# Retention and a squared-ReLU feed-forward on one core: feed-forward on one 128-token unit, and an order from a list schedule

## The chip, the core and the metric

The kernel runs on one core of a Trainium2 chip. The metric is the device time of one execution in microseconds (us), the median of several runs. The core's engines work through their own instruction streams in order: TensorE (PE, with weight loads shown apart as PEld), VectorE (DVE), ScalarE (ACT), GpSimd (POOL) and SyncE (SP), which issues the loads from memory. They wait for one another by semaphores.

## The reference

The input holds q, k and v of 8 batches, 8 heads, 576 positions and 64 dimensions, and two weight matrices. The first half is causal retention with a decay per head, the second a feed-forward with squared ReLU:

```python
scores = q @ k.T / sqrt(64)                    # per batch and head
ret = scores * where(i >= j, gamma[h] ** (i - j), 0)
x = (ret @ v), heads side by side              # 4608 tokens x 512
h = x @ w_in                                   # 512 x 2048
out = max(h, 0) ** 2 @ w_out                   # 2048 x 512, float32 out
```

The kernel casts to float16 for the matmuls and sums in float32.

## The kernel before, in words

The 4608 tokens are cut into 36 units of 128. Of each batch, units c = 0 to 3 are chunks of 128 positions ("full"); the last 64 positions of two batches share a "tail" unit. So five units in nine are: four of one batch, four of the next and a tail, with 8 full units of c = 0, 24 others and 4 tails.

**Retention of a unit.** The loads of q, k, v (L69, tails L72) are 256 KB each. `cast_unit` casts k on POOL (L171) and q on DVE for units 0 to 7, on POOL for later ones (L172), and multiplies v by a decay on POOL (L175). On PE, `steps_T` transposes k and q with 4 matmuls each of 128 columns (L191) into one PSUM tile, `psT`; after the last of the 8, ACT copies k to `kTb` in two halves (L196, L197) and DVE copies q to `qT` (L198). `steps_score` makes 8 score matmuls (L215) and DVE applies the mask in two operations (L218). `steps_state` (4 matmuls, L240) carries the state R from chunk to chunk (DVE: L246 for c = 0, else L249 and L250). `steps_out` multiplies scores with v (8 matmuls, L268) and adds the state's share (none for c = 0, 4 matmuls for other full units, 8 of 64 columns for a tail, L274); DVE scales it into `xT` (L281). All of these matmuls have 128 or 64 moving columns and a weight load of their own.

**Feed-forward of a group.** Four units make a group of 512 tokens. `steps_ff1` takes each of 16 slices f of the hidden dimension: 4 matmuls of 512 columns (L301) into one PSUM bank `ph`, then ReLU on ACT (L306) and the square on DVE (L307) into `gT`. `steps_ff2` takes each unit of the group: 16 matmuls of 512 columns (L326) into `po`, a copy on ACT (L330) and the store, issued by ACT (L333). `ph` and `po` share three PSUM banks.

**What sets the order.** The tile pools keep the program's order on each engine (`manual_schedule`). The retention of units 0 to 3 runs first, one unit after another; then the four blocks of w_in are cast on DVE (`cast_w`, L97) while the loads of w_out wait for the four staging buffers that these casts free; then the feed-forward of group 0 runs, with the casts of w_out ahead of its second half; then the retention of units 4 to 7, one after another. From group 1 on, the loop at the end puts one or two retention steps of the units of the next group behind each feed-forward matmul, at phases written by hand (`SLOT`, `late`). Constants (`lnrow`, `gam`, masks) are made at the start; DVE also clears `bdec` and three sets of `vp` and `kTb` (L156, L159, L160) before its first cast of q.

Of the kernel before, what the change touches and what calls it, by code (L numbers as in the profile page):

```python
# [11 lines left out]
ALU = mybir.AluOpType  # L12


@with_exitstack
def kernel(
# [43 lines left out]

    loaded = {}

    def load(u):
        kind, b, c = units[u]
        t = {}
        for name, src in (("q", q), ("k", k), ("v", v)):
            x = ld.tile([P, H, D], FP32, name=f"{name}32", tag=f"{name}32")
            if kind == "full":
                nc.sync.dma_start(out=x, in_=src[b, :, c * P:(c + 1) * P, :].rearrange("h p d -> p h d"))  # L69
            else:  # L70
                for i in range(2):
                    nc.sync.dma_start(out=x[i * 64:(i + 1) * 64],  # L72
                                      in_=src[b + i, :, 512:576, :].rearrange("h p d -> p h d"))
            t[name] = x
        loaded[u] = t
# [4 lines left out]
    NLD = 6  # L80
    for u in range(UPG):
        load(u)
    w_st = []
    for fb in range(4):
        t = stage.tile([P, NP, 512], FP32, name=f"wi{fb}", tag="wst")
        nc.sync.dma_start(out=t, in_=w_in[:, fb * 512:(fb + 1) * 512].rearrange("(m p) f -> p m f", p=P))
        w_st.append(t)

    def load_w_out(fb):
        t = stage.tile([P, 4, DM], FP32, name=f"wo{fb}", tag="wst")  # L90
        nc.sync.dma_start(out=t, in_=w_out[fb * 512:(fb + 1) * 512, :].rearrange("(n p) m -> p n m", p=P))
        w_st.append(t)

    def cast_w(i):
        fb = i % 4
        dst = w_in16[:, :, fb * 512:(fb + 1) * 512] if i < 4 else w_out16[:, fb * 4:(fb + 1) * 4, :]
        nc.vector.tensor_copy(out=dst, in_=w_st[i])  # L97
# [53 lines left out]
    NB = 3  # L151
# [12 lines left out]
    ret = {}  # L164

    def cast_unit(u):
        kind = units[u][0]
        t = loaded.pop(u)
        k16 = cast.tile([P, H * D], FP16, name="k16", tag="k16")
        q16 = cast.tile([P, H * D], FP16, name="q16", tag="q16")  # L170
        nc.gpsimd.tensor_copy(out=k16, in_=t["k"].rearrange("p h d -> p (h d)"))  # L171
        (nc.vector if u < 2 * UPG else nc.gpsimd).tensor_copy(out=q16, in_=t["q"].rearrange("p h d -> p (h d)"))  # L172
        vp = vps[u % NB]
        vo = vp.rearrange("p n (a d) -> p n a d", d=64)[:, :, 0:3:2, :]
        nc.gpsimd.tensor_tensor(  # L175
            out=vo,
            in0=t["v"].rearrange("p (n a) d -> p n a d", a=2),
            in1=vdec[kind].rearrange("p (n a o) -> p n a o", a=2, o=1).to_broadcast([P, NP, 2, D]),
            op=ALU.mult)
        ret[u] = {"k16": k16, "q16": q16, "vp": vp}  # L180

    def steps_T(u):
        r = ret[u]
        steps = []
        for i, src in enumerate(("k16", "q16")):
            for hp in range(NP):
                def f(i=i, src=src, hp=hp):
                    if i == 0 and hp == 0:
                        r["psT"] = ps_one.tile([P, 2, NP, P], FP16, name="psT", tag="psT")
                    ps = r["psT"]  # L190
                    nc.tensor.transpose(ps[:, i, hp, :], r[src][:, hp * P:(hp + 1) * P], ident)  # L191
                    if hp == NP - 1:
                        if i == 1:
                            kT = kTs[u % NB]
                            qT = work.tile([P, NP, P], FP16, name="qT", tag="qT")
                            nc.scalar.copy(out=kT[0:64, :, 0, :], in_=ps[0:64, 0])  # L196
                            nc.scalar.copy(out=kT[64:128, :, 1, :], in_=ps[64:128, 0])  # L197
                            nc.vector.tensor_copy(out=qT, in_=ps[:, 1])  # L198
                            r["kT"], r["qT"] = kT, qT
                steps.append(f)  # L200
        return steps

    def steps_score(u):
        kind = units[u][0]
        r = ret[u]
        steps = []
        for hp in range(NP):
            for a in range(2):
                def f(hp=hp, a=a):
                    if hp == 0 and a == 0:  # L210
                        r["rT"] = work.tile([P, NP, 2, P], FP16, name="rT", tag="rT")
                    rT = r["rT"]
                    if hp % 2 == 0 and a == 0:
                        r["psc"] = ps_sc.tile([P, 2, 2, P], FP32, name="psc", tag="psc")
                    nc.tensor.matmul(r["psc"][:, hp % 2, a, :], lhsT=r["kT"][:, hp, a, :],  # L215
                                     rhs=r["qT"][:, hp, :], start=True, stop=True)
                    if hp % 2 == 1 and a == 1:
                        nc.vector.tensor_tensor(  # L218
                            out=rT[:, hp - 1:hp + 1].rearrange("p n a i -> p (n a) i"),
                            in0=r["psc"].rearrange("p n a i -> p (n a) i"),  # L220
                            in1=mask[kind].rearrange("p (o i) -> p o i", o=1).to_broadcast([P, 4, P]),
                            op=ALU.mult)
                steps.append(f)
        return steps

    R = {}

    def steps_state(u):
        kind, b, c = units[u]
        if kind == "tail":  # L230
            return []
        r = ret[u]
        steps = []
        for hp in range(NP):
            def f(hp=hp):
                if hp == 0:
                    r["psS"] = ps_one.tile([P, NP, 2, D], FP32, name="psS", tag="psS")
                ps = r["psS"]
                vo = r["vp"].rearrange("p n (a d) -> p n a d", d=64)[:, hp, 0:3:2, :]
                nc.tensor.matmul(ps[:, hp], lhsT=r["k16"][:, hp * P:(hp + 1) * P], rhs=vo,  # L240
                                 start=True, stop=True)
                if hp == NP - 1:
                    psf = ps.rearrange("p n a d -> p n (a d)")
                    Rn = st_pool.tile([P, NP, P], FP16, name="R", tag="R")
                    if c == 0:
                        nc.vector.tensor_tensor(out=Rn, in0=psf, in1=bdec, op=ALU.mult)  # L246
                    else:
                        tmp = work.tile([P, NP, P], FP32, name="stmp", tag="stmp")
                        nc.vector.tensor_tensor(out=tmp, in0=psf, in1=R[b], op=ALU.add)  # L249
                        nc.vector.tensor_tensor(out=Rn, in0=tmp, in1=bdec, op=ALU.mult)  # L250
                    r["Rn"] = Rn
            steps.append(f)
        return steps

    xTs = {}

    def steps_out(u):
        kind, b, c = units[u]
        r = ret[u]
        g, s = divmod(u, UPG)  # L260
        inter = [] if c == 0 else ([(0, P, R[b])] if kind == "full" else [(0, 64, R[b]), (64, P, R[b + 1])])
        steps = []
        for hp in range(NP):
            for a in range(2):
                def f(hp=hp, a=a):
                    if hp == 0 and a == 0:
                        r["psO"] = ps_one.tile([P, NP, P], FP32, name="psO", tag="psO")
                    nc.tensor.matmul(r["psO"][:, hp, :], lhsT=r["vp"][:, hp, a * 64:a * 64 + P],  # L268
                                     rhs=r["rT"][:, hp, a, :], start=(a == 0),
                                     stop=(a == 1 and not inter))  # L270
                steps.append(f)
            for i, (lo, hi, Rb) in enumerate(inter):
                def f(hp=hp, lo=lo, hi=hi, Rb=Rb, last=(i == len(inter) - 1)):
                    nc.tensor.matmul(r["psO"][:, hp, lo:hi], lhsT=Rb[:, hp, :], rhs=r["qT"][:, hp, lo:hi],  # L274
                                     start=False, stop=last)
                steps.append(f)
# [153 lines left out]
```

## Time and profile before

| | |
|---|---|
| median of 3 runs | 373.37 us |
| the runs | 371.81, 373.37, 375.94 us |
| the profiled execution | 375.74 us, its span 374.0 us |
| mean granted TensorE clock | 0.938 |
| DMA | 46.52 MB, 36.70 MB read, mean 124 GB/s |

The span is the time from the first to the last instruction of the profiled execution. A line of a timeline begins with the start, then the time that the merged instructions took together, the engine, the line of the kernel, and the number of instructions; brackets hold the idle time ahead of it and what ended it. A line of a table of stretches gives for each engine the busy time and, in brackets, the number of instructions, then the granted TensorE clock (1.00 is full), the busy share of the DMA engines and GB/s. Matmuls are pipelined: the distance between the starts of two tells what one costs in a run of them, not its own length.

### The profile page before, as it was taken

Reading aid. Unit: us, or ns where it says so; the run is one execution under the profiler, and the core shown is the slowest. Engines: PE = TensorE matmul, PEld = TensorE weight load, DVE = VectorE, ACT = ScalarE, POOL = GpSimd, SP = SyncE. Lnnn points to the kernel's source line nnn. Section 1 sums busy time; section 2 is a strip of 40 time slices with the busy share of each in tenths; the row PEclk is TensorE's granted clock in tenths of the full one; section 3 lists DMA queues with packets and bytes.
Section 4 is the critical chain, followed back from the end, with each engine's and each line's share of the span. In section 5 each row is a group of like instructions: output and inputs, shape, how many; then the busy total and the mean of one; then the engine's idle time right before and its main releaser. Section 6 shows DMA issues by size and latency. Waiting matters only on the chain.

```text
span 374.0 us, 5968 instructions
## 1 busy us (share of the span) xinstructions
PE 332.7 (89%) x2272; PEld 186.3 (50%) x2272; DVE 207.1 (55%) x401; ACT 151.4 (40%) x259; POOL 84.1 (22%) x113
## 2 busy tenths in 40 slices
PE   0565979654899999999999999999999999999995
PEld 0453434344555555555555555555555555555442
DVE  5477565174468547645744784485368637832400
ACT  3211540312164256435632652465356236523621
POOL 4500024042323222223222322222223222000000
PEclk9986798955599999999999999999999999999999
DMA  9990999598985554555355436545300020011012
GB/s 175 253 358 9 359 256 190 172 220 148 222 142 113 154 154 94 116 141 133 86 124 151 119 86 142 150 104 118 109 29 2 28 58 28 2 58 58 0 53 60
DMA packets 122012, 46.52 MB, mean 124 GB/s; under 512 B 113280, under 2 KB 113280, under 8 KB 121984
## 3 DMA queue, kind: packets, MB, share of 16 engines
q1 hardware_dynamic: 116736, 36.71, 45.3%
q10 hardware_dynamic: 5248, 9.44, 7.3%
q8 instruction: 17, 0.28, 0.3%
q14 instruction: 11, 0.09, 0.1%
HBM read 36.70 MB, written 9.44 MB: 123 GB/s over the span
## 4 chain that ended last, share of the span: by engine, by line
PE 84%; DVE 10%; ACT 4%; issue 1%; ACTq 0%
PE ph L301 34%; PE po L326 34%; PE psc L215 5%; PE psT L191 4%; PE psO L268 4%; DVE rT L218 2%; PE psS L240 2%; ACT kTb L197 1%; ACT kTb L196 1%; DVE xT L281 1%; PE psO L274 1%; DVE R L250 1%; DVE qT L198 1%; DVE stmp L249 1%; DVE q L172 1%
## 5 line engine op out<-in xcount | busy, mean ns | idle before, releaser
L301 PE MATMUL ph<-xT,w_in 128*128 128x512 f16 x576 | 155.9, 389 | 3.3 <-DVE w_in L97 2.2
L326 PE MATMUL po<-w_out,gT 128*128 128x512 f16 x576 | 150.9, 383 | 2.6 <-DVE w_out L97 2.4
L306 ACT ACTIVATE rl<-ph 128x512 f16<-128x512 f32 x144 | 85.7, 597 | 60.4 <-PE ph L301 54.0
L307 DVE TENSOR_TENSOR gT<-rl 128x512 f16<-128x512 f16 x144 | 67.3, 472 | 48.3 <-ACT rl L306 47.5
L301 PEld LDWEIGHTS <-w_in 128*128 128x128 f16 x576 | 55.9, 100 | 53.4 <-issue 7.4
L326 PEld LDWEIGHTS <-gT 128*128 128x128 f16 x576 | 55.0, 99 | 52.0 <-DVE w_out L97 2.9
L215 PE MATMUL psc<-qT,kTb 128*128 128x128 f16 x288 | 55.9, 234 | 14.8 <-DVE qT L198 14.8
L330 ACT COPY o<-po 128x512 f32<-128x512 f32 x36 | 21.1, 586 | 108.6 <-PE po L326 107.0
L175 POOL TENSOR_TENSOR vp<-v,vdec_full 128x512 f16<-128x512 f32 x32 | 36.2, 1133 | 106.6 <-PE psO L274 45.3
L198 DVE COPY qT<-psT 128x512 f16<-128x512 f16 x36 | 15.3, 425 | 66.6 <-ACT kTb L197 66.6
L218 DVE TENSOR_TENSOR rT<-psc,mask_full 128x512 f16<-128x512 f32 x64 | 43.0, 685 | 9.5 <-PE psc L215 9.5
L171 POOL CAST k<-k 128x512 f16<-128x512 f32 x36 | 23.2, 644 | 108.9 <-DMA k<-in_k_dram 53.0
L268 PE MATMUL psO<-rT,vp 128*128 128x128 f16 x288 | 46.9, 236 | 0.6 <-DVE rT L218 0.6
L196 ACT COPY kTb<-psT 64x512 f16<-64x512 f16 x36 | 20.8, 579 | 47.8 <-PE psT L191 44.9
L215 PEld LDWEIGHTS <-kTb 128*128 128x128 f16 x288 | 28.1, 105 | 19.3 <-ACT kTb L196 7.9
L268 PEld LDWEIGHTS <-vp 128*128 128x128 f16 x288 | 29.5, 106 | 14.9 <-issue 1.1
L191 PE MATMUL psT<-ident,q 128*128 128x128 f16 x144 | 20.3, 234 | 9.4 <-DVE q L172 9.4
L274 PE MATMUL psO<-qT,R 128*128 128x128 f16 (+1 forms) x128 | 27.0, 230 | 0.0
L191 PE MATMUL psT<-ident,k 128*128 128x128 f16 x144 | 20.7, 238 | 6.0 <-POOL k L171 6.0
L240 PE MATMUL psS<-vp,k 128*128 128x128 f16 x128 | 25.8, 240 | 0.0
L191 PEld LDWEIGHTS <-k 128*128 128x128 f16 x144 | 14.5, 108 | 17.0 <-POOL k L171 6.0
L191 PEld LDWEIGHTS <-q 128*128 128x128 f16 x144 | 13.6, 104 | 17.5 <-DVE q L172 11.1
(47 smaller groups left out, 170.3 us busy)
## 6 DMA issues: line engine op xcount, KB each, us to landing
q<-in_q_dram SPq DMA_DIRECT2D x32, 256.0 KB, 3.6
k<-in_k_dram SPq DMA_DIRECT2D x32, 256.0 KB, 4.5
v<-in_v_dram SPq DMA_DIRECT2D x32, 256.0 KB, 4.1
out_dram<-o ACTq DMA_DIRECT2D x32, 256.0 KB, 2.3
wi<-in_moe_w_in_dram SPq DMA_DIRECT2D x4, 1024.0 KB, 9.1
wo<-in_moe_w_out_dram SPq DMA_DIRECT2D x4, 1024.0 KB, 8.6
q<-in_q_dram SPq DMA_DIRECT2D x8, 128.0 KB, 3.7
k<-in_k_dram SPq DMA_DIRECT2D x8, 128.0 KB, 3.9
```

Source lines behind the costliest of these rows:

```text
L175: nc.gpsimd.tensor_tensor(out=vo, in0=t["v"].rearrange("p (n a) d -> p n a d", a=2), in1=vdec[kind].rearrange("p (n a o) -> p n a o", a=2, ...
L191: nc.tensor.transpose(ps[:, i, hp, :], r[src][:, hp * P:(hp + 1) * P], ident)
L196: nc.scalar.copy(out=kT[0:64, :, 0, :], in_=ps[0:64, 0])
L215: nc.tensor.matmul(r["psc"][:, hp % 2, a, :], lhsT=r["kT"][:, hp, a, :], rhs=r["qT"][:, hp, :], start=True, stop=True)
L218: nc.vector.tensor_tensor(out=rT[:, hp - 1:hp + 1].rearrange("p n a i -> p (n a) i"), in0=r["psc"].rearrange("p n a i -> p (n a) i"), in1= ...
L240: nc.tensor.matmul(ps[:, hp], lhsT=r["k16"][:, hp * P:(hp + 1) * P], rhs=vo, start=True, stop=True)
L268: nc.tensor.matmul(r["psO"][:, hp, :], lhsT=r["vp"][:, hp, a * 64:a * 64 + P], rhs=r["rT"][:, hp, a, :], start=(a == 0), stop=(a == 1 and ...
L274: nc.tensor.matmul(r["psO"][:, hp, lo:hi], lhsT=Rb[:, hp, :], rhs=r["qT"][:, hp, lo:hi], start=False, stop=last)
L301: nc.tensor.matmul(cur["ph"], lhsT=w_in16[:, m, f * P:(f + 1) * P], rhs=xTs[g][:, m, :], start=(m == 0), stop=(m == NP - 1))
L306: nc.scalar.activation(out=rl, in_=cur["ph"], func=ACTF.Relu)
L307: nc.vector.tensor_tensor(out=gT[f], in0=rl, in1=rl, op=ALU.mult)
L326: nc.tensor.matmul(po[t], lhsT=gT[f][:, t * P:(t + 1) * P], rhs=w_out16[:, f, :], start=(f == 0), stop=(f == NF - 1))
```

## The change

The feed-forward works on one unit of 128 tokens instead of a group of four. FFN1 of a unit takes four slices f into the four quarters of one PSUM bank, so each of its matmuls has 128 moving columns instead of 512 and there are 2304 of them instead of 576; ReLU and square still take 512 columns at a time, four of each per unit. FFN2 is the same 16 matmuls of 512 columns per unit.

All of the work after the constants is given as tasks to a new class, `Schedule`: each has an engine, a key, a duration, tasks that it depends on, and counted resources that it takes (PSUM banks, buffers). `emit` plays an event simulation with these durations and a latency per engine; whenever an engine is free it starts the ready task with the smallest key whose resources are there. The order of the starts is the program's order. Keys are places in units of 32 feed-forward slots: the feed-forward of unit u lies at 32u, its retention from 32(u - 1) - 17.6 on. The simulation starts with all engines free at time 0; the constants are not in it.

Other edits: loads go k, q, v; the order of the loads is units 0 to 3, the eight weight blocks, units 4 and on. Staging has 5 buffers instead of 4, the loads of units 5 instead of 6, `vp` and `kTb` 4 instead of 3, and other pools change size. Each weight block is cast half on DVE and half on ACT, with a key ahead of nearly all other work. The copies of k wait for the transposes of k alone. q is cast on DVE for units 0 to 3 only. The bodies of the retention's instructions are as before. The core of the diff:

```diff
+class Schedule:
+    LAT = {"PE": 0.25, "ACT": 0.12, "DVE": 0.12, "POOL": 0.15, "SP": 2.0}
+    def __init__(self, count):
+        self.count = dict(count)
+        self.tasks = []
+    def add(self, eng, key, dur, fn, deps=(), acq=(), after=None):
+        t = dict(eng=eng, key=key, dur=dur, fn=fn, acq=acq, n=len(self.tasks), users=[], free=[],
+                 left=len(deps), ready=0.0, lat=self.LAT[eng] if after is None else after)
+        for d in deps:
+            d["users"].append(t)
+        self.tasks.append(t)
+        return t
+    def free(self, res, tasks):
+        group = dict(res=res, left=len(tasks))
+        for t in tasks:
+            t["free"].append(group)
...
+            for e in ready:
+                if busy[e]:
+                    continue
+                held = []
+                while ready[e]:
+                    item = heapq.heappop(ready[e])
+                    t = item[2]
+                    if all(self.count[r] > 0 for r in t["acq"]):
+                        for r in t["acq"]:
+                            self.count[r] -= 1
+                        t["start"] = now
+                        order.append(t)
+                        busy[e] = True
+                        push(now + t["dur"], "end", t)
+                        break
+                    held.append(item)
...
+                if what == "end":
+                    busy[t["eng"]] = False
+                    for w in t["users"]:
+                        push(now + (0.0 if w["eng"] == t["eng"] else t["lat"]), "dep", w)
+                    for g in t["free"]:
+                        push(now + t["lat"], "free", g)
...
+        for t in order:
+            t["fn"]()
...
-    UPG = 4
-    NG = NU // UPG
     const = ctx.enter_context(tc.tile_pool(name="const", bufs=1))
-    ld = ctx.enter_context(tc.tile_pool(name="ld", bufs=6))
-    stage = ctx.enter_context(tc.tile_pool(name="stage", bufs=4))
-    cast = ctx.enter_context(tc.tile_pool(name="cast", bufs=3))
-    work = ctx.enter_context(tc.tile_pool(name="work", bufs=2))
-    st_pool = ctx.enter_context(tc.tile_pool(name="st", bufs=4))
-    g_pool = ctx.enter_context(tc.tile_pool(name="g", bufs=2))
+    ld = ctx.enter_context(tc.tile_pool(name="ld", bufs=5))
+    stage = ctx.enter_context(tc.tile_pool(name="stage", bufs=5))
+    cast = ctx.enter_context(tc.tile_pool(name="cast", bufs=4))
+    work = ctx.enter_context(tc.tile_pool(name="work", bufs=3))
+    o_pool = ctx.enter_context(tc.tile_pool(name="o", bufs=2))
+    x_pool = ctx.enter_context(tc.tile_pool(name="x", bufs=5))
+    st_pool = ctx.enter_context(tc.tile_pool(name="st", bufs=6))
+    g_pool = ctx.enter_context(tc.tile_pool(name="g", bufs=16))
     r_pool = ctx.enter_context(tc.tile_pool(name="r", bufs=3))
     ps_ff = ctx.enter_context(tc.tile_pool(name="ps_ff", bufs=3, space=bass.MemoryType.PSUM))
...
-    NB = 3
+    NB = 4
...
+    sched = Schedule(dict(ph=2, po=1, psc=2, psT=1, psS=1, psO=1, ld=5, wst=5, k16=4, q16=4,
+                          qT=3, rT=3, x=5, g=4, rl=3, o=2, R=6))
+    add = sched.add
+    tile_of = {}
+    last_load = []
+    def dma_task(key, dur, fn, **kw):
+        t = add("SP", key, dur, fn, deps=list(last_load), **kw)
+        last_load[:] = [t]
+        return t
...
+        for n, (name, src) in enumerate((("k", k), ("q", q), ("v", v))):
+            def fn(name=name, src=src):
...
+            loaded[name, u] = dma_task(0, 1.22, fn, acq=("ld",) if n == 0 else ())
+    def add_weight(i):
+        fb = i % 4
...
+        t = dma_task(0, 2.75, fn, acq=("wst",))
+        dst = w_in16[:, :, fb * 512:(fb + 1) * 512] if i < 4 else w_out16[:, fb * 4:(fb + 1) * 4, :]
+        halves = []
+        for j, eng in enumerate(("DVE", "ACT")):
+            def fc(j=j, eng=eng):
+                s = tile_of["w", i]
+                (nc.vector.tensor_copy if eng == "DVE" else nc.scalar.copy)(
+                    out=dst[:, 2 * j:2 * j + 2], in_=s[:, 2 * j:2 * j + 2])
+            halves.append(add(eng, -50 + i, 0.65 if eng == "DVE" else 1.0, fc, deps=[t]))
+        sched.free("wst", halves)
+        wcast[i] = halves
+    ahead = 4
+    for u in range(ahead):
+        add_load(u)
+    for i in range(8):
+        add_weight(i)
+    for u in range(ahead, NU):
+        add_load(u)
+    T = {}
+    L = 2 * NF
+    def add_ret(u):
+        kind, b, c = units[u]
+        base = (u - 1) * L
...
+        ck = add("POOL", base - L, 0.73, fk, deps=[loaded["k", u]], acq=("k16",))
+        if u < ahead:
+            cq = add("DVE", base - L, 0.42, fq, deps=[loaded["q", u]], acq=("q16",))
+        else:
+            cq = add("POOL", base - L + 1, 0.62, fq, deps=[loaded["q", u]], acq=("q16",))
+        cv = add("POOL", base - L + 2, 1.1, fv, deps=[loaded["v", u]] + ([T["out", u - NB]] if u >= NB else []))
+        sched.free("ld", [ck, cq, cv])
...
+        tk = add("PE", base - 17.6, 0.22, ft(0, "k16"), deps=[ck], acq=("psT",))
+        tq = add("PE", base - 15.6, 0.22, ft(1, "q16"), deps=[cq, tk])
+        sched.free("q16", [tq])
+        kT = kTs[u % NB]
...
+        prev = [T["score", u - NB]] if u >= NB else []
+        e0 = add("ACT", base - 15.5, 0.58, fe0, deps=[tk] + prev)
+        e1 = add("ACT", base - 15.4, 0.58, fe1, deps=[tk] + prev)
+        eq = add("DVE", base - 15.3, 0.42, feq, deps=[tq], acq=("qT",))
+        sched.free("psT", [e0, e1, eq])
...
+            s = add("PE", base + 0.5, 0.22, fs, deps=[ck, cv], acq=("psS",))
+            sched.free("k16", [s, tk])
...
+                sc.append(add("PE", base + 5 + 2 * half + j + 0.6, 0.11, f, deps=[e0, e1, eq] + sc[-1:],
+                              acq=("psc",) if j == 0 else ()))
...
+            ms.append(add("DVE", base + 7 + 2 * half, 0.7, fm, deps=[sc[-1]] + ms[-1:],
+                          acq=("rT",) if half == 0 else ()))
+            sched.free("psc", [ms[-1]])
...
+            outs.append(add("PE", base + 18.5 + hp, 0.16, f,
+                            deps=[ms[hp // 2], cv] + [T["R", ru] for _, _, ru in inter] + outs[-1:],
+                            acq=("psO",) if hp == 0 else ()))
...
+        T["x", u] = add("DVE", base + 22.6, 0.7, fx, deps=[outs[-1]], acq=("x",))
+        sched.free("psO", [T["x", u]])
+        T["out", u] = outs[-1]
...
+    def add_ff(u):
+        base = u * L
+        f1 = []
+        sq = []
+        for fb in range(4):
+            for j in range(4):
+                def f(fb=fb, j=j):
+                    if j == 0:
+                        tile_of["ph", u, fb] = ps_ff.tile([P, 4, P], FP32, name="ph", tag="ff")
+                    fi = 4 * fb + j
+                    for m in range(NP):
+                        nc.tensor.matmul(tile_of["ph", u, fb][:, j, :], lhsT=w_in16[:, m, fi * P:(fi + 1) * P],
+                                         rhs=tile_of["x", u][:, m, :], start=(m == 0), stop=(m == NP - 1))
+                acq = ()
+                if j == 0:
+                    acq = ("ph", "g") if fb == 0 else ("ph",)
+                f1.append(add("PE", base + 4 * fb + j, 0.216, f, deps=[T["x", u]] + wcast[fb] + f1[-1:], acq=acq))
+            def fr(fb=fb):
+                t = tile_of["rl", u, fb] = r_pool.tile([P, 4, P], FP16, name="rl", tag="rl")
+                nc.scalar.activation(out=t, in_=tile_of["ph", u, fb], func=ACTF.Relu)
+            def fg(fb=fb):
+                t = tile_of["g", u, fb] = g_pool.tile([P, 4, P], FP16, name="gT", tag="gT")
+                rl = tile_of["rl", u, fb]
+                nc.vector.tensor_tensor(out=t, in0=rl, in1=rl, op=ALU.mult)
+            r = add("ACT", base + 4 * fb + 4, 0.6, fr, deps=[f1[-1]], acq=("rl",))
+            sched.free("ph", [r])
+            sq.append(add("DVE", base + 4 * fb + 6, 0.45, fg, deps=[r]))
+            sched.free("rl", [sq[-1]])
+        sched.free("x", [f1[-1]])
+        f2 = []
+        for fi in range(NF):
+            def f(fi=fi):
+                if fi == 0:
+                    tile_of["po", u] = ps_ff.tile([P, DM], FP32, name="po", tag="ff")
+                nc.tensor.matmul(tile_of["po", u], lhsT=tile_of["g", u, fi // 4][:, fi % 4, :], rhs=w_out16[:, fi, :],
+                                 start=(fi == 0), stop=(fi == NF - 1))
+            f2.append(add("PE", base + NF + fi, 0.216, f, deps=[sq[fi // 4]] + wcast[4 + fi // 4] + f2[-1:],
+                          acq=("po",) if fi == 0 else ()))
+        sched.free("g", [f2[-1]])
...
+        oc = add("ACT", base + L + 1, 0.59, fo, deps=[f2[-1]], acq=("o",))
+        sched.free("po", [oc])
+        st = add("ACT", base + L + 1.1, 0.05, fd, deps=[oc], after=2.5)
+        sched.free("o", [st])
+    for u in range(NU):
+        add_ret(u)
+    for u in range(NU):
+        if ("Rread", u) in T:
+            sched.free("R", T["Rread", u])
+    for u in range(NU):
+        add_ff(u)
+    sched.emit()
```

More of the change, by code (lines that the diff above doesn't have):

```diff
@@ L1 @@
+import heapq
 import math
@@ L161 @@
         kTs.append(t)
[L164 to L224, printed above, removed]
@@ L236, in f @@
                 if hp == 0:
[L237 to L257, printed above, removed]
-        kind, b, c = units[u]
[L259 to L276, printed above, removed]
-        def fin():
-            if s == 0:
-                xTs[g] = work.tile([P, NP, UPG * P], FP16, name="xT", tag="xT")
-            nc.vector.tensor_tensor(out=xTs[g][:, :, s * P:(s + 1) * P], in0=r["psO"], in1=gam[kind], op=ALU.mult)
-            if "Rn" in r:
-                R[b] = r["Rn"]
-            del ret[u]
-        last = steps[-1]
-        steps[-1] = lambda: (last(), fin())
-        return steps
@@ L342, in run @@
-    def run(steps):
-        for s in steps:
-            s()
-    def whole(u):
-        cast_unit(u)
-        if u + NLD < NU and u >= UPG:
-            load(u + NLD)
-        run(steps_T(u))
-        run(steps_score(u))
-        run(steps_state(u))
-        run(steps_out(u))
-    for u in range(UPG):
-        whole(u)
-    for i in range(4):
-        cast_w(i)
-        load_w_out(i)
-    for u in range(UPG, UPG + NLD):
-        load(u)
-    run(steps_ff1(0))
-    run(steps_ff2(0))
-    for u in range(UPG, 2 * UPG):
-        whole(u)
@@ new lines, in f @@
+                ps = tile_of["psO", u]
+                for a in range(2):
+                    nc.tensor.matmul(ps[:, hp, :], lhsT=vps[u % NB][:, hp, a * 64:a * 64 + P],
+                                     rhs=tile_of["rT", u][:, hp, a, :], start=(a == 0),
+                                     stop=(a == 1 and not inter))
+                for n, (lo, hi, ru) in enumerate(inter):
+                    nc.tensor.matmul(ps[:, hp, lo:hi], lhsT=tile_of["R", ru][:, hp, :],
+                                     rhs=tile_of["qT", u][:, hp, lo:hi], start=False, stop=(n == len(inter) - 1))
```

270 lines of the change are left out of this document (156 added, 114 removed).

## The prediction

> **What bounds the kernel now.** I read the page first, then a table of stretches cut where TensorE changes its work, then the timeline of PE.
>
> ```profile
> span 374.0 us, 5968 instructions
> PEclk9986798955599999999999999999999999999999
> PE 84%; DVE 10%; ACT 4%; issue 1%; ACTq 0%
> ```
>
> PE carries 84% of the chain that ended last, yet its clock is low in the first quarter. The stretches say which quarter is at fault (retention of units 0 to 3; feed-forward of group 0; retention of units 4 to 7; the start of group 1; the rest; the drain):
>
> ```profile
> 0.00:35.58 35.58, 14.58 (x125) 12.24 (x125) 21.59 (x70) 7.58 (x15) 9.02 (x21) 0.89 0.85 207
> 35.58:70.65 35.07, 32.46 (x129) 13.53 (x129) 17.54 (x24) 11.31 (x19) 6.70 (x6) 0.87 0.94 232
> 70.65:97.36 26.71, 13.86 (x126) 11.80 (x125) 15.82 (x26) 5.23 (x9) 8.84 (x11) 0.59 1.09 202
> 97.36:103.94 6.58, 6.30 (x23) 2.77 (x23) 1.33 (x3) 2.78 (x5) 1.47 (x3) 0.59 1.28 218
> 103.94:369.60 265.66, 265.55 (x1874) 145.93 (x1873) 150.84 (x279) 124.03 (x212) 58.03 (x73) 1.00 0.36 90
> 369.60:374.00 4.40, 0.00 (x0) 0.00 (x0) 0.00 (x0) 0.51 (x1) 0.00 (x0) 0.82 0.27 60
> ```
>
> From 103.94 on PE is always busy at clock 1.00. "Busy" alone proves nothing for pipelined matmuls, so I price them by the distance between starts:
>
> ```profile
> 11.91 1.01 PE L215 MATMUL psc<-qT,kTb 128*128 128x128 f16 x8 [1.73 <-DVE qT L198]
> 35.58 16.79 PE L301 MATMUL ph<-xT,w_in 128*128 128x512 f16 x64 [2.22 <-DVE w_in L97]
> ...
> 73.54 0.61 PE L215 MATMUL psc<-qT,kTb 128*128 128x128 f16 x8 [2.28 <-DVE qT L198]
> 73.98 0.39 PE L240 MATMUL psS<-vp,k 128*128 128x128 f16 x4
> ...
> 341.70 13.98 PE L301 MATMUL ph<-xT,w_in 128*128 128x512 f16 x64
> 355.51 13.98 PE L326 MATMUL po<-w_out,gT 128*128 128x512 f16 x64
> ```
>
> The 64 matmuls of 512 columns from 341.70 to 355.51 cost 13.81/64 = 0.2158 us each. The eight of 128 columns at 73.54 took 0.61, the four behind them 0.39: the four more cost 0.22, so one costs 0.055; I use (0.61 - 0.39)/4 rounded up, 0.0556, which also makes four of them 0.2224 against 0.2158. The first line, at half clock, is some (1.01 - 0.61)/7 = 0.06 dearer per matmul. The trace's whole middle agrees (all PE, then L301, then L326):
>
> ```profile
> 120.00:320.00 200.00, 200.00 (x1466) 112.30 (x1464) 121.48 (x220) 94.78 (x161) 53.54 (x68) 1.00 0.40 99
> 120.00:320.00 200.00, 99.73 (x367) 34.44 (x367) 1.00 0.40 99
> 120.00:320.00 200.00, 102.00 (x377) 35.24 (x375) 1.00 0.40 99
> ```
>
> 744 x 0.2158 + 722 x 0.0556 = 200.7 us of work in 200 us. So the middle has no stall left to remove: only the first 104 us and the drain have. The reader can check what is there: 124 retention matmuls, 6.9 us at full clock, take 26.7 us from 70.65 on, and as many are most of the first 35.58.
>
> **Part 1: FFN1 in 128 columns.** 576 matmuls of 0.2158 become 2304 of 0.0556: 124.3 becomes 128.1 us, plus 3.8. There are 1728 more weight loads. They are hidden if a load runs beside the matmul ahead of it. The rows:
>
> ```profile
> 73.54 0.43 PEld L215 LDWEIGHTS <-kTb 128*128 128x128 f16 x7 [0.97 <-ACT kTb L197]
> 73.93 0.27 PEld L240 LDWEIGHTS <-k 128*128 128x128 f16 x4
> L301 PEld LDWEIGHTS <-w_in 128*128 128x128 f16 x435 | 41.0, 98 | 30.9 <-issue 0.6 <-DVE xT L281 0.4
> ```
>
> A load lasts 98 ns alone, but seven take 0.43, four 0.27: one per 0.055, in step with the matmuls. Nothing longer than these 12 in a row is in the trace. Bounds: 0.0556 and, were each load exposed, 0.098 (plus 97.7 us). I take 0.0556, since rows of exactly this shape say so; no gain is possible, as the columns streamed stay the same.
>
> The Trainium skill ("TensorE: Matmul & The Clock Gate", section "Back-to-back issue gap") speaks against the change: it gives a sustained 81 ns for a stream of weight load and 128-column matmul, and calls 56 ns the gap of isolated ones. By that figure FFN1 would take 186.6 us, 58.5 more than my term. The 12 matmuls at 73.54 contradict it as far as they go.
>
> ReLU, square, copy and store keep their shapes and counts (144, 144, 36), as do the retention's. The chain that the two `ph` banks allow: a full bank costs 16 x 0.0556 = 0.89. A bank's refill must wait for its ReLU.
>
> ```profile
> L306 ACT ACTIVATE rl<-ph 128x512 f16<-128x512 f32 x110 | 65.4, 597 | 34.7 <-PE ph L301 28.4 <-DVE gT L307 2.4 <-PE psS L240 2.4
> L196 ACT COPY kTb<-psT 64x512 f16<-64x512 f16 x27 | 15.6, 579 | 9.7 <-PE psT L191 7.2 <-issue 2.5
> ```
>
> Last start to end 0.22 (0.61 - 7 x 0.0556), ReLU 0.60, some 0.1 for two semaphores: 0.92, against 0.0556 + 0.89 = 0.95 of cover by the other bank. It just fits; hidden, with 0.03 to spare, unless ACT does something else first. ACT's two copies of k are 1.16 together, but their keys (15.5 ahead of the retention's base) lie behind the last fill of FFN1, where FFN2's 16 x 0.2158 = 3.45 covers them. I take 2 us of stalls over 36 units; bounds 0 and 11 (0.3 per unit, a quarter of the two copies).
>
> **Part 2: the head.** When can FFN1 start? It needs x of unit 0, block 0 of w_in, and its cast. The loads' queue, and what the DMA moved meanwhile (last column, GB/s):
>
> ```profile
> 0.81 0.43 SPq L69 DMA_DIRECT2D q<-in_q_dram  x1
> 13.50 2.93 SPq L86 DMA_DIRECT2D wi<-in_moe_w_in_dram  x4
> 35.55 3.77 SPq L91 DMA_DIRECT2D wo<-in_moe_w_out_dram  x4
> ```
>
> ```profile
> 20.00:26.00 6.00, 3.14 (x32) 2.79 (x30) 3.58 (x7) 1.16 (x2) 0.00 (x0) 0.85 1.05 386
> 28.00:35.00 7.00, 3.00 (x28) 2.53 (x28) 4.73 (x9) 1.16 (x2) 0.00 (x0) 0.72 0.00 1
> ```
>
> And what DVE does before the first cast of weights, with POOL's cast of q for later:
>
> ```profile
> 8.34 0.17 DVE L156 MEMSET vp<- 128x128 uint32 x1
> 9.16 0.35 DVE L172 CAST q<-q 128x512 f16<-128x512 f32 x1
> 17.51 0.42 DVE L198 COPY qT<-psT 128x512 f16<-128x512 f16 x1 [1.92 <-ACT kTb L197]
> 18.61 1.29 DVE L218 TENSOR_TENSOR rT<-psc,mask_full 128x512 f16<-128x512 f32 x2 [0.68 <-PE psc L215]
> 19.82 0.68 DVE L249 TENSOR_TENSOR stmp<-psS,R 128x512 f32<-128x512 f32 x1
> 20.53 0.69 DVE L250 TENSOR_TENSOR R<-stmp,bdec 128x512 f16<-128x512 f32 x1
> 21.14 0.68 DVE L281 TENSOR_TENSOR xT<-psO,gam_full 128x512 f16<-128x512 f32 x1
> 21.74 0.42 DVE L172 CAST q<-q 128x512 f16<-128x512 f32 x1
> 34.30 4.62 DVE L97 CAST w_in<-wi 128x2048 f16<-128x2048 f32 x4
> ...
> L172 POOL CAST q<-q 128x512 f16<-128x512 f32 x24 | 17.3, 721 | 0.0
> ```
>
> Weights come at 386 GB/s, 2.7 us a block; the four blocks end by 28 and took 10.9, so the first landed by 20. But before, its cast stands on DVE behind four whole retentions, at 34.30, and w_out is not even issued until 35.55: DMA idles from 28 to 35. After, the cast goes ahead and the queue runs on. What decides is then DVE. The fourth set of `vp` and `kTb` adds one set's 0.82 (8.34 to 9.16): DVE begins with q at 10.0. A unit costs it 0.42 + 0.42 + 1.29 + 0.68 + 0.69 + 0.68 = 4.2 us, four 16.1 (unit 0 lacks one operation). In the schedule's own clock unit 0's q starts at 4.4 (2 x 1.22 + 2.0) and the first weight block is there at 19.4 (12 x 1.22 + 2.75 + 2.0): what DVE starts in those 15 stands ahead of the cast. That clock is only the order; on the chip this stretch begins at 10.0 instead of 4.4, so the cast comes near 25, and half a block takes 4.62/8 = 0.58. ACT's half is at most two 512-column copies, 1.2. I put FFN1's start at **26**; bounds 22 (weights landed, casts) and 31 (halfway from 26 to today's 35.58, the pace of retentions in series).
>
> Two new waits are hidden. DVE would wait for a block with the rest of the retentions behind it, and PE for those; but the blocks land from 20 on, 2.7 apart, 5 us ahead of DVE. SP waits for a staging buffer at its sixth block, with two blocks and unit 4's loads behind; its turn is near 20 + 4 x 2.7 = 31, and block 0's casts free a buffer near 27.
>
> From there PE should have work always: feed-forward of units 0 to 3 is 28 us, to 54 at least; w_out's blocks land by 20 + 7 x 2.7 = 39, before FFN2's turn near 43; unit 4's loads, behind them, need 3.6 us (786 KB at 218 GB/s), and a retention some 7, so its x is there near 50. POOL's q casts for units 4 to 7 hide behind the same 4 us; if that cover is gone they cost 0.7 once. Two losses remain. The clock: FFN1 begun cold took 16.79 at 35.58 and 13.98 at 341.70, so 2.8 (0 to 5). And ACT: 16 ReLUs of 0.60 and five or six half blocks of up to 1.2 are some 16 us beside 14.3 of PE, so 2 (0 to 5).
>
> **Part 3: the drain** keeps its last copy and store: 4.4.
>
> **The sum**, from FFN1's start: FFN1 128.1; FFN2 576 x 0.2158 = 124.3; retention of units 4 to 35, 1120 - 124 = 996 matmuls, 55.4, less 0.9 for 32 half-width ones, 54.5; together 306.9.
>
> 26 + 306.9 + 2.8 + 2 + 2 + 4.4 = 344.1 us of span. The other way round: 374.0 less 9.6 (start), 35.07 - 128 x 0.2158 = 7.5 (group 0), 26.7 - 6.8 = 19.9 (second retention), about 3 (cold start of group 1) and 1.4 (the gap before it) plus 3.8 for FFN1 and the 6.8 of losses comes to 343.2. The profiled execution took 375.74, 1.74 beyond its span: 345.8 after. It lies high among the runs (371.81 to 375.94); scaled to their median, 345.8 x 373.37/375.74 = 343.7, so **344 us**.
>
> **Rivals.** *A, weight loads exposed (slower).* In runs of 16 and more the loads could fall behind, since each lasts 98 ns and only 12 in a row are seen hidden. Place: all of FFN1. Price: 2304 x 0.042 = 97.7, giving 441. It decides from 29.4/2304 = 0.013 per matmul, above 0.068 each; below that the change still wins. Against it: two loads overlap in the rows above. Chance 0.06 (the skill's 81 ns would give 402).
>
> *B, the order doesn't fit the chip.* PE runs in order, and a wait that the schedule's rough latencies miss holds all behind it: a ReLU behind both k copies makes PE stand 1.16 - 0.03 = 1.13. At every unit 41 us: 385; at one in three 13.6: 358. For it: two banks leave 0.03. Against it: of the 8.7 us that PE needs per unit (313.8/36, with the first four retentions), ACT needs 8.7 x 94.78/200 = 4.1 and DVE 5.3 by the middle's row. Chance 0.15, at 358.
>
> *C, the head's order gains little.* If FFN1 starts only at 35.58 because casts and retentions interlock on DVE: 344 + 9.6 = 354. Against it: the loads run on. Chance 0.12.
>
> **How the numbers follow.** Forecast 0.67, A 0.06, B 0.15, C 0.12. Low: 22 + 306.9 + 4.4 + 1.7 = 335.0, scaled 333. High: 31 + 306.9 + 5 + 5 + 11 + 4.4 + 1.7 = 365.0, scaled 363; it takes in C and B at one in three. Within 1% (about what a measurement of this kernel can tell) needs B at nearly every unit: 0.02. Slower by more than 1%: A and the worst of B, 0.07. Faster 0.91.
>
> **What would show it.** Right: PE's first L301-like matmul near 26, starts 0.056 apart over runs of 16, clock 1.00 from about 30, no idle gap over 1 us afterwards, the last matmul near 339. Wrong: starts 0.07 apart or more (A); PE idle behind ACT's ReLU once per unit (B); DVE still on retention at 30 with the weights landed (C).

## The result, and the profile after

The changed kernel takes **355.08 us** (median of 4 runs, 354.23 to 355.97) against 373.22 us before (4 runs): a ratio of 0.951, 95% interval 0.944 to 0.957. The direction was forecast and the time lies in the range, but 11 us above the 344 given as likeliest. The runs come in two pairs, 354.23 and 354.32 against 355.84 and 355.97; the profiled execution is the one of 354.32 us, with a span of 352.6.

The page, lines that answer to those of before:

```profile
span 352.6 us, 9372 instructions
PE 325.5 (92%) x4000; PEld 250.7 (71%) x4000; DVE 192.4 (55%) x400; ACT 155.3 (44%) x267; POOL 83.3 (24%) x117
...
PE 86%; ACT 6%; DVE 4%; issue 1%; DVEq 0%
```

PE is busier, yet ACT now has 6% of the chain that ended last, against 4%. A table of stretches (the head up to the first FFN1 matmul; the feed-forward of the first units; the rest; the drain):

```profile
0.00:27.15 27.15, 12.00 (x113) 10.41 (x113) 18.89 (x68) 8.62 (x16) 9.31 (x21) 1.00 1.09 268
27.15:59.95 32.80, 32.53 (x396) 24.81 (x397) 19.58 (x36) 20.21 (x32) 11.48 (x14) 1.00 1.10 283
59.95:348.20 288.25, 280.99 (x3495) 215.44 (x3492) 153.96 (x297) 126.27 (x220) 62.50 (x82) 1.00 0.43 104
348.20:352.60 4.40, 0.00 (x0) 0.00 (x0) 0.00 (x0) 0.20 (x1) 0.00 (x0) 0.86 0.28 61
```

FFN1 starts at 27.15 instead of 35.58, and the second retention stretch (26.7 us before) is gone. But the long stretch, where PE was always busy before, now leaves 288.25 - 280.99 = 7.3 us idle. The list of PE's waits says where:

```profile
PE psT L307 <- ACT kTb L316: 6.8, 30, 0.2
PE psT L307 <- DVE q L283: 5.3, 1, 5.3
PE psT L307 <- POOL k L279: 5.0, 1, 5.0
```

Each line gives the total in us, the number of waits and the longest: thirty waits of the transposes on ACT's first copy of k, 0.2 us each; the other two lines are single waits in the head. PE's list has no wait on ReLU. One unit on PE's timeline (L307 transposes, L441 FFN1, L466 FFN2):

```profile
199.32 0.39 PE L307 MATMUL psT<-ident,k 128*128 128x128 f16 x4
199.55 0.39 PE L441 MATMUL ph<-xT,w_in 128*128 128x128 f16 x4
199.77 0.38 PE L466 MATMUL po<-w_out,gT 128*128 128x512 f16 x1
200.38 0.38 PE L307 MATMUL psT<-ident,q 128*128 128x128 f16 x4 [0.23 <-ACT kTb L316]
200.60 0.59 PE L466 MATMUL po<-w_out,gT 128*128 128x512 f16 x2
```

and the same moment on ACT:

```profile
199.75 0.58 ACT L316 COPY kTb<-psT 64x512 f16<-64x512 f16 x1 [0.30 <-PE psT L307]
200.23 0.59 ACT L450 ACTIVATE rl<-ph 128x512 f16<-128x512 f32 x1
201.32 0.58 ACT L319 COPY kTb<-psT 64x512 f16<-64x512 f16 x1 [0.50 <-DVE qT L323]
```

k's transposes end at 199.71, ACT copies from 199.75 to 200.33, and only then, at 200.38, do q's transposes start, though q was cast long before (POOL's last cast of a q ran at 191.68): they write the PSUM tile `psT` that ACT is reading. Even ACT's second copy waits for DVE's copy of q out of that tile. The bracket says 0.23 idle, but the matmul ahead, of 512 columns, should be followed after 0.216; the start comes 0.61 behind it, so 0.39 is lost. The bracket counts only from the end that the profile gives to the matmul ahead (it shows 0.38 for a matmul that another can follow after 0.216). The thirty gaps are alike to 0.01 us and cost 11.7 us where the profile's idle time is 6.8.

The account for the profiled execution: 27.15 to FFN1, 308.3 of work at the measured distances (0.0558 and 0.2159, and 12 retention matmuls that were left when FFN1 began), 11.7 in those gaps, 0.4 in one other gap (ahead of the matmul at 34.51), and 5.0 from 0.2159 behind the last matmul's start to the end of the span: 352.6.

### The profile page after: what moved, and what is told of

Its sections match the earlier page's. It is cut to its first block, busy times and chain, and to the rows that moved or that the text cites. A ratio compares the mean times of both kernels' runs of the same rounds, so it can differ in the third digit from the quotient of the medians.

```text
span 352.6 us, 9372 instructions
## 1 busy us (share of the span) xinstructions
PE 325.5 (92%) x4000; PEld 250.7 (71%) x4000; DVE 192.4 (55%) x400; ACT 155.3 (44%) x267; POOL 83.3 (24%) x117
## 4 chain that ended last, share of the span: by engine, by line
PE 86%; ACT 6%; DVE 4%; issue 1%; DVEq 0%
PE ph L441 34%; PE po L466 33%; PE psT L307 6%; ACT kTb L316 5%; PE psc L375 5%; PE psO L407 5%; PE psS L336 2%; PE psO L411 2%; DVE stmp L350 1%; DVE rT L383 1%; DVE w_in L256 0%; DVE R L355 0%; ACT kTb L319 0%; ACT gam_full L186 0%; DVE kTb L206 0%
## 5 line engine op out<-in xcount | busy, mean ns | idle before, releaser
L441 PE MATMUL ph<-xT,w_in 128*128 128x128 f16 x2304 | 158.3, 219 | 0.7 <-DVE w_in L256 0.7
L466 PE MATMUL po<-w_out,gT 128*128 128x512 f16 x576 | 155.0, 379 | 0.0
L441 PEld LDWEIGHTS <-w_in 128*128 128x128 f16 x2304 | 139.4, 98 | 9.6 <-DVE w_in L256 1.1
L466 PEld LDWEIGHTS <-gT 128*128 128x128 f16 x576 | 53.3, 98 | 36.3
L283 POOL CAST q<-q 128x512 f16<-128x512 f32 x32 | 19.8, 619 | 103.8 <-PE psT L307 60.0
L288 POOL TENSOR_TENSOR vp<-v,vdec_full 128x512 f16<-128x512 f32 x32 | 34.2, 1069 | 36.2 <-PE psO L411 23.7
L375 PE MATMUL psc<-qT,kTb 128*128 128x128 f16 x288 | 38.4, 226 | 1.7 <-DVE qT L323 1.7
L279 POOL CAST k<-k 128x512 f16<-128x512 f32 x36 | 23.3, 647 | 70.5 <-DMA k<-in_k_dram 31.6
L407 PE MATMUL psO<-rT,vp 128*128 128x128 f16 x288 | 39.5, 224 | 0.0
L350 DVE TENSOR_TENSOR stmp<-psS,R 128x512 f32<-128x512 f32 x24 | 16.6, 690 | 38.4 <-PE psS L336 38.4
L423 DVE TENSOR_TENSOR xT<-psO,gam_full 128x512 f16<-128x512 f32 x32 | 22.1, 691 | 21.5 <-PE psO L411 18.0
L319 ACT COPY kTb<-psT 64x512 f16<-64x512 f16 x36 | 20.9, 580 | 20.5 <-DVE qT L323 15.2
L316 ACT COPY kTb<-psT 64x512 f16<-64x512 f16 x36 | 20.8, 578 | 20.6 <-PE psT L307 20.1
L307 PEld LDWEIGHTS <-q 128*128 128x128 f16 x144 | 11.2, 99 | 24.2 <-issue 17.5
L307 PE MATMUL psT<-ident,q 128*128 128x128 f16 x144 | 14.4, 224 | 14.8 <-ACT kTb L316 6.8
```

Of the source, the lines that this page charges most:

```text
L279: nc.gpsimd.tensor_copy(out=t, in_=tile_of["k32", u].rearrange("p h d -> p (h d)"))
L288: nc.gpsimd.tensor_tensor(out=vo, in0=tile_of["v32", u].rearrange("p (n a) d -> p n a d", a=2), in1=vdec[kind].rearrange("p (n a o) -> p n ...
L307: nc.tensor.transpose(tile_of["psT", u][:, i, hp, :], tile_of[src, u][:, hp * P:(hp + 1) * P], ident)
L316: nc.scalar.copy(out=kT[0:64, :, 0, :], in_=tile_of["psT", u][0:64, 0])
L375: nc.tensor.matmul(tile_of["psc", u, half][:, j, a, :], lhsT=kT[:, hp, a, :], rhs=tile_of["qT", u][:, hp, :], start=True, stop=True)
L407: nc.tensor.matmul(ps[:, hp, :], lhsT=vps[u % NB][:, hp, a * 64:a * 64 + P], rhs=tile_of["rT", u][:, hp, a, :], start=(a == 0), stop=(a == ...
```

## The experiments

**Theory.** The transposes of q and the copies out of the same PSUM tile shut each other out. Before, all eight transposes came first; the new order puts ACT's first copy between k's and q's. **Rivals.** The missing time is spread over many small waits or over exposed weight loads in FFN1; or the wait only moves when its place changes.

**E1: q's transposes right behind k's**

```diff
-        tq = add("PE", base - 15.6, 0.22, ft(1, "q16"), deps=[cq, tk])
+        tq = add("PE", base - 17.5, 0.22, ft(1, "q16"), deps=[cq, tk])
```

> One number is changed against the changed kernel: the key of q's transposes goes from 15.6 to 17.5 slots ahead of the unit's base, so that they stand right behind k's transposes in the order, ahead of ACT's first copy of k out of the same PSUM tile. Theory 1 (the wait on one PSUM bank): q's transposes write the bank that ACT is reading, and stand still 0.395 us in 30 units; with the new order PE never waits there, 11.8 us go, and the time falls from 355 to 343 us (341 to 345). Theory 2 (the missing 11 us are spread over the order's many small waits, or over exposed weight loads in FFN1): under 2 us change, 353 to 355. Theory 3 (the wait only moves, since the copies of k now wait for q's transposes and with them everything behind on ACT): 349 to 355, with PE idle before another line.

Measured: 342.76 us (342.52 to 345.16), ratio to before 0.920 (0.915 to 0.926): 12.3 us off the changed kernel. PE's timeline of one unit:

```profile
213.40 0.39 PE L307 MATMUL psT<-ident,k 128*128 128x128 f16 x4
213.63 0.39 PE L307 MATMUL psT<-ident,q 128*128 128x128 f16 x4
213.85 0.39 PE L441 MATMUL ph<-xT,w_in 128*128 128x128 f16 x4
214.07 0.81 PE L466 MATMUL po<-w_out,gT 128*128 128x512 f16 x3
```

None of the thirty gaps is left, here or in PE's list of waits. The wait does move, but to where it costs nothing: ACT's first copy of k waits for the transposes for 26.8 us in all instead of 20.1, DVE's copy of q waits for ACT's first copy (30 times, 18.8 us), and both engines have time. The order on ACT, DVE and POOL is that of the changed kernel. From the first FFN1 matmul of unit 5 to that of unit 35 (69.47 to 331.23) 261.76 us pass, against 273.00 in the changed kernel (67.59 to 340.59): 11.24 less, about what the 29 gaps in this stretch cost (0.39 each). Theories 2 and 3 fall.

**E2: the order as it is, q's transposes in another bank**

```diff
+                tag = "psS" if i else "psT"
+                tile_of["psT", u, i] = ps_one.tile([P, 2, NP, P], FP16, name=tag + "t", tag=tag)
...
+        tq = add("PE", base - 15.6, 0.22, ft(1, "q16"), deps=[cq, tk], acq=("psS",))
```

The state matmuls' bank is free at that time; the schedule counts it for both.

> The order's keys stay as in the changed kernel, but q's transposes go to the PSUM bank that the state matmuls use instead of k's. Theory 1 (one bank): nothing is left to wait for, though ACT's copy of k still stands ahead of q's transposes: 343 us (341 to 346), and ACT's second copy no longer waits for DVE's copy of q. If instead the place in the order itself or ACT's pace is to blame, 353 to 356 as before.

Measured: 341.20 us (340.85 to 342.90), ratio 0.916 (0.910 to 0.921). The same moment on PE, and on ACT:

```profile
201.21 0.39 PE L307 MATMUL psTt<-ident,k 128*128 128x128 f16 x4
201.43 0.39 PE L442 MATMUL ph<-xT,w_in 128*128 128x128 f16 x4
201.65 0.38 PE L467 MATMUL po<-w_out,gT 128*128 128x512 f16 x1
201.87 0.39 PE L307 MATMUL psSt<-ident,q 128*128 128x128 f16 x4
```

```profile
201.63 0.58 ACT L316 COPY kTb<-psTt 64x512 f16<-64x512 f16 x1 [0.29 <-PE psTt L307]
202.11 0.59 ACT L451 ACTIVATE rl<-ph 128x512 f16<-128x512 f32 x1
202.73 0.58 ACT L319 COPY kTb<-psTt 64x512 f16<-64x512 f16 x1
```

Here ACT's copy runs from 201.63 to 202.21 and q's transposes start at 201.87, in its middle, 0.22 behind the FFN2 matmul. The schedule counts the second bank and so moves a few tasks in the first 67 us (FFN1 starts at 26.03 instead of 27.15); behind that the order on every engine is that of the changed kernel, and only the bank differs. From unit 5 to unit 35 the same 261.76 us pass as in E1 (66.08 to 327.84). So the place in the order alone does not make the wait, and neither does ACT's pace; it takes the shared tile, with ACT's first copy ahead of q's transposes. ACT's second copy has lost its wait on DVE too. Whether the chip itself needs the wait inside one bank was not tried: no run takes the wait alone away. The Trainium skill ("PSUM — Partial Sum Buffer", section "PSUM bank collisions raise a hardware error") says that two engines must be kept apart by bank and quadrant, not by address, with no arbitration by the chip; what the program does in E2 and in the changed kernel agrees with this, and no run here shows the collision.

**E3: the kernel before, with FFN1 in 128 columns alone**

```diff
-                    nc.tensor.matmul(cur["ph"], lhsT=w_in16[:, m, f * P:(f + 1) * P], rhs=xTs[g][:, m, :],
-                                     start=(m == 0), stop=(m == NP - 1))
+                    for n in range(NP):
+                        nc.tensor.matmul(cur["ph"][:, m * P:(m + 1) * P], lhsT=w_in16[:, n, f * P:(f + 1) * P],
+                                         rhs=xTs[g][:, n, m * P:(m + 1) * P],
+                                         start=(n == 0), stop=(n == NP - 1))
```

> The kernel before with one part of the change alone: FFN1's matmuls take 128 columns instead of 512, each with its weight load, four times as many, in the old order. Loads hidden: 128 against 124.3 us in FFN1, so 373.2 + 3.8 = 377 us (375 to 380). Loads exposed as in rival A, or at 81 ns each: 430 us or more.

Measured: 376.67 us, ratio 1.011 (1.003 to 1.018): 3.5 us more than the 373.13 beside it, with an interval of 1 to 7 us; the spacing in the trace is the sharper measure. In its last group FFN1 runs 256 such matmuls in a row:

```profile
340.95 14.46 PE L302 MATMUL ph<-xT,w_in 128*128 128x128 f16 x256
355.24 13.98 PE L328 MATMUL po<-w_out,gT 128*128 128x512 f16 x64
```

(355.24 - 340.95)/256 = 0.0558 us each, every one with a weight load of its own. Rival A of the prediction falls. The 81 ns that the Trainium skill gives for such a stream ("TensorE: Matmul & The Clock Gate", section "Back-to-back issue gap") are not what this shape costs here.

**E4: the weights' casts behind the retention of unit 3**

```diff
-            halves.append(add(eng, -50 + i, 0.65 if eng == "DVE" else 1.0, fc, deps=[t]))
+            halves.append(add(eng, 90 + i, 0.65 if eng == "DVE" else 1.0, fc, deps=[t]))
```

> The changed kernel with the weights' casts keyed behind the retention of unit 3 (key 90 on instead of -50 on), as they stood in the kernel before. If the head gains because the casts pass the retention on DVE, FFN1 starts 4 to 6 us later than its 27.15 and the time is 360 us (358 to 363). If FFN1's start hangs on x or on the loads instead, nothing changes: 354 to 356.

Measured: 357.51 us (355.93 to 357.95), 2.4 above the changed kernel (the intervals of the two ratios, 0.952 to 0.963 and 0.944 to 0.957, overlap a little): between the two forecasts, and too little for the first. FFN1's start:

```profile
28.55 0.22 PE L411 MATMUL psO<-qT,R 128*128 128x128 f16 x1
28.60 0.27 PE L407 MATMUL psO<-rT,vp 128*128 128x128 f16 x2
28.71 0.22 PE L411 MATMUL psO<-qT,R 128*128 128x128 f16 x1
29.04 6.70 PE L441 MATMUL ph<-xT,w_in 128*128 128x128 f16 x112
```

All four retentions end at 28.9 here, with no weight cast ahead of the work that they wait for, where before their last matmul started at 33.04. So passing the retention gives the casts some 2 us (27.15 to 29.04), perhaps a little more, since in E4's profile the matmuls of the head are 0.056 apart from 17 us on and in the changed kernel's only from 25 us on. The other 6.5 of the 8.4 us by which FFN1 starts earlier are still there in E4. Of these, 4.3 lie in the retentions (last matmul at 33.04 before, 28.71 here), which now stand in one another's waits, and 2.2 in the shorter way from there to FFN1 (2.5 to 0.3), where the casts are split between two engines. These two causes are argued, not tried alone; and part of the 4.3 is TensorE's rate, since in the kernel before the matmuls still started 0.107 apart just ahead of 33 us.

**E5, E6, E7: the head, on top of E2.** E5 clears three of the four sets of `vp` and `kTb` on POOL; E6 also casts q of units 0 to 3 on ACT; E7 is E2 with the simulation told when each engine is free after the constants. The diff has their parts in this order, new lines only (the clears of `kTb` change like that of `vp`). These three ran beside other runs of the kernel before, with a median of 372.59 instead of 373.13. From unit 5 to unit 35 each of them takes the 261.76 us of E1 and E2, so what sets them apart lies ahead of unit 5.

```diff
+        (nc.gpsimd if i else nc.vector).memset(t[:, :, 64:128], 0.0)
...
+            (nc.scalar.copy if u < ahead else nc.gpsimd.tensor_copy)(
...
+        for e, at in (("DVE", 10.4), ("ACT", 4.1), ("POOL", 3.0), ("SP", 1.0)):
+            busy[e] = True
+            push(at, "end", dict(eng=e, users=[], free=[]))
```

> On top of the kernel with q's transposes in a bank of their own: three of the four sets of vp and kTb are cleared on POOL instead of DVE, which takes 2.6 us of clearing off DVE before its first cast of q. If DVE's work from its first cast on sets when FFN1 can start, FFN1 starts near 23.5 instead of 26.0, and the time falls from 341.2 to 338.7 us (338 to 340). If the landing of the first weights or the retention's chain of waits sets it, under 0.7 us change.

Measured: 339.33 us (339.20 to 341.08), 1.9 below E2 and in the range forecast for DVE as the limit, though the 95% intervals of the two ratios (0.909 to 0.916, 0.910 to 0.921) overlap. FFN1 starts at 25.27 and not at 23.5, in a profile where its first matmuls are still 0.107 apart. DVE gets to its first cast 2.8 us earlier, but the cast then takes twice as long, 2.06 instead of 1.02 in E2 at 10.44:

```profile
7.42 0.27 DVE L206 MEMSET kTb<- 64x256 uint32 x1
7.62 2.06 DVE L283 CAST q<-q 128x512 f16<-128x512 f32 x1
10.39 0.42 DVE L323 COPY qT<-psSt 128x512 f16<-128x512 f16 x1 [0.70 <-PE psSt L307]
```

With POOL idle such a cast takes 0.42; both of these run beside work of POOL. So the time agrees with DVE as the limit of the head, but the sum of its durations alone does not tell when FFN1 starts.

> As the run before, and q of units 0 to 3 is cast on ACT instead of DVE: 4 x 0.42 = 1.7 us less for DVE in the head, 4 x 0.59 us more for ACT, which idles there for three quarters. If DVE still sets FFN1's start: 1 to 1.7 us earlier again, 337 to 338 us. If the chain through PE and ACT or the weights do, no change or up to 1 us slower.

Measured: 339.49 us (339.42 to 339.64): no change against E5. FFN1 starts at 23.06, but FFN2 then stands before the first block of w_out:

```profile
23.06 1.96 PE L442 MATMUL ph<-xT,w_in 128*128 128x128 f16 x32 [1.30 <-DVE w_in L256]
...
26.42 5.74 PE L442 MATMUL ph<-xT,w_in 128*128 128x128 f16 x96
32.67 1.04 PE L467 MATMUL po<-w_out,gT 128*128 128x512 f16 x4 [0.51 <-DVE w_out L256]
```

DVE's work no longer decides alone; the weights and their casts come up beside it. What the earlier start itself is worth stays open, since the two profiles differ in TensorE's rate too: E6's matmuls are 0.056 apart from 14 us on, E5's only from 26.7.

> The kernel with q's transposes in a bank of their own, and the schedule's simulation told when the engines are really free after the constants (DVE 10.4, ACT 4.1, POOL 3.0, SP 1.0 us) instead of all at 0. If the misfit of the head's order costs time, FFN1 starts 1 us or more before 26.0 and the time is 340 us or less; if the order doesn't matter there because DVE's total work does, 340.7 to 342.

Measured: 340.41 us (340.19 to 342.25), 0.8 below E2, between the two forecasts, and an amount that the 95% intervals of the two ratios (0.910 to 0.921, 0.911 to 0.918) do not tell from nothing. Yet FFN1 starts at 20.86, 5 us earlier, with 40 instead of 12 retention matmuls still to do. The early start is given back in new gaps:

```profile
20.86 2.04 PE L445 MATMUL ph<-xT,w_in 128*128 128x128 f16 x32 [0.72 <-DVE w_in L259]
...
24.04 2.20 PE L445 MATMUL ph<-xT,w_in 128*128 128x128 f16 x32 [0.59 <-DVE w_in L259]
...
32.61 1.04 PE L470 MATMUL po<-w_out,gT 128*128 128x512 f16 x4 [0.51 <-DVE w_out L259]
```

By the medians, then, the misfit of the simulation's clock is worth under 1 us. E5 and E6, the fastest kernels here, take 0.91 of the time before (0.909 to 0.916, 0.908 to 0.915).

## Why the prediction was right in direction and 11 us short

**Part 1, price of 128 columns: right.** 0.0556 was read from 12 matmuls in a row; 256 in a row (E3) cost 0.0558, and E3's whole step is 3.5 us (1 to 7) against 3.8 predicted.

**Part 1, stalls over the units: wrong, and this is the step that failed.** The prediction looked for stalls where ReLU meets two `ph` banks, found 0.03 us to spare and took "2 us of stalls over 36 units; bounds 0 and 11". ReLU never stopped PE. The stall came from an edit that it did not price: in the new code the copies of k wait for the transposes of k alone, and so stand ahead of q's transposes in the order. It cost 11.7 us, just past the bound, and E1 and E2 each take it away (12.3 and 13.9 us by the medians). A row that could have told it is on the page of before: DVE's copy of q was always held until ACT's copy of k had ended, 66.6 us in all, though the two read different halves of `psT`:

```profile
L198 DVE COPY qT<-psT 128x512 f16<-128x512 f16 x36 | 15.3, 425 | 66.6 <-ACT kTb L197 66.6
```

That is one tile shutting out its users. Rival B named the mechanism (PE held in order behind a wait that the schedule doesn't know) and a size close to the measured one (358), at the wrong place: behind ACT's ReLU, where PE never stood, instead of ACT's copy. The schedule's list of what an instruction waits for lacks the shared tile.

**Part 2, FFN1's start: 26 predicted, 27.15 measured.** DVE came to its casts of q at 10.43 (10.0 predicted) and to its first cast of w_in at 26.40 (25 predicted), behind which FFN1 starts. From 20 to 30 us it was busy for 9.54 of 10 us (third pair of numbers):

```profile
26.40 0.68 DVE L256 CAST w_in<-wi 128x1024 f16<-128x1024 f32 x1
...
20.00:30.00 10.00, 7.67 (x105) 7.26 (x106) 9.54 (x18) 4.49 (x7) 0.00 (x0) 1.00 1.05 386
```

From 10.43 to 20 it was busy for only 5.88 of 9.57 us, so waits on PE and ACT set a part of the pace. E4 shows that the reason given, the casts passing the retention, carries only some 2 us; more goes with the overlap of the retentions. And E7 shows that FFN1's start is a poor measure when work is left behind.

**Part 2, clock and ACT.** The profiled execution lost nothing to the clock in FFN1 (48 matmuls in 2.85 us from 27.15) and 0.4 to ACT and DVE, instead of 2.8 and 2.

**The conversion.** The profiled execution of before lay above its median, and the prediction scaled its sum down by as much, 345.8 to 343.7. After, the profiled execution lay 0.8 below the median. Of the 11 us between 344 and 355, about 8.5 are in the span (11.7 of gaps, 1.2 of start, 1.4 of work and 0.6 of drain more; 6.4 of forecast losses less) and the rest is this conversion. That the miss is no larger, and the time inside the range, is partly luck: losses of 6.4 us that were put in did not come, and hid about half of a stall that was not put in. The range's upper end did hold 11 us of stalls, but for another wait.

Rival C (354 us) came close in time, for a reason that did not occur: FFN1 did not start at 35.58.

## What to carry to other kernels

When work is put in a new order, list for each PSUM tile who writes and who reads it, and keep a second writer ahead of the first reader or give it another bank; a planner that counts buffers but not this can place the wait in the middle of the busiest engine, as it did here. Price a stall of a pipelined engine by the distance between starts, since the idle time shown (6.8 us) can be little more than half of what is lost (11.7). And splitting 512 columns into four of 128 with their own weight loads cost 3% of FFN1's time, so a finer unit can pay where it fills an empty head.

## What the runs showed of the hardware that was not expected

- DVE's casts and copies and POOL's work hold one another up. A cast of q from float32 on DVE took 0.42 us in every profile where POOL stood idle. Beside POOL the first one took 1.02 in E1, E2 and E4, and 2.06 in E5, where it ended 0.28 us after the last of three POOL instructions in a row. In the changed kernel it was the other way round: the cast at 10.43 took its 0.35, and POOL's multiplication beside it 1.39 instead of 1.04:

```profile
10.43 0.35 DVE L283 CAST q<-q 128x512 f16<-128x512 f32 x1
...
10.30 1.39 POOL L288 TENSOR_TENSOR vp<-v,vdec_full 128x512 f16<-128x512 f32 x1 [1.87 <-DMA v<-in_v_dram]
```

- The column of the granted clock reads 1.00 for the whole head of the changed kernel, yet matmuls of 128 columns start 0.107 apart there (eight took 1.01 us at 17.46) and 0.056 apart from 25 us on. The trace's first record of the clock is at 23.7 us, and ahead of it the column says nothing: there the spacing, not the column, tells the rate.
- When the rate changes differs from profile to profile: the last matmuls 0.107 apart start at 13.9 us in E6, 15.1 in E2, 23.3 in the changed kernel, 26.5 in E5 and 29.1 in E1. In E1 and E5 this takes in the first FFN1 matmuls: the first 48 took 3.19 and 3.51 us there, against 2.85 in the changed kernel. What sets the moment is not settled here.
